# Softmax normalised in the exponent, spectrum and its swapped copy in one slot, and new instruction orders, in a four-layer attention and state-space kernel

## The chip, the cores and the metric

The kernel runs on one core of one Trainium2 chip. The metric is device time in microseconds (us) of one execution. The engines are named as the profile names them: PE (TensorE, matmuls), PEld (its weight loads), DVE (VectorE), ACT (ScalarE), POOL (GpSimd) and SP (SyncE, which issues nearly all DMAs).

## The reference, cut to what matters

Four residual layers on x of 2048 rows by 512 columns in bf16: attention (A), long convolution (B), A, B, each fed by a layer norm. The same weights serve both layers of a kind.

```python
def A(x, wqkv, wo):                      # 32 heads of 16, window of 8 keys, every second row
    q, k, v = split(x @ wqkv)
    idx = pos[:, None] - 2 * arange(8)[None, :]
    logits = einsum("bhsd,bhswd->bhsw", q, k[idx]) * 16 ** -0.5    # -1e9 where idx < 0
    return einsum("bhsw,bhswd->bhsd", softmax(logits), v[idx]) @ wo

def B(u, A_re, A_im, B_re, B_im, C_re, C_im, log_dt, Dskip):
    K = einsum("dn,dnl,dn->dl", C, exp(dt * A * l), dt * B).real   # 512 kernels of length 2048
    return irfft(rfft(u, 4096) * rfft(K, 4096))[:2048] + u * Dskip

x = x + A(layernorm(x)); x = x + B(layernorm(x))
x = x + A(layernorm(x)); x = x + B(layernorm(x))
```

## The kernel before, in words

Everything stays in SBUF between the layers; the residual is `x_sb`, 128 partitions by 16 rows by 512. There is no scheduler at work: `manual_schedule` keeps each engine's instructions in the order in which Python emits them, and that order comes from strings of letters. `ORDERK` orders the first stage, `CORE0` and `CORE1` the two attention layers, `ORDER0`, `ORDERF` and `ORDER1` the two convolutions and the way from the first to the second attention layer. One letter is one piece of work: usually a few matmuls and the instruction that empties their PSUM tile. Because each engine takes its queue in order, a letter's place decides what its instructions wait behind.

Five stages follow each other:

- **First stage** (`k_gen`, `ORDERK`). The convolution kernel K is made from powers of exp(dt A), by complex products on DVE (`tt`, L1108) and matmuls (`product`, L1266); the layer norm, the transposes and the q and k projections of the first attention layer run beside it.
- **First attention core** (`core`, `CORE0`). For each of four blocks of 512 rows: `mult` (L340) forms the products of q with eight shifted views of k on DVE, four instructions of 4096 elements; `lsum` (L348, L352) sums them on PE into a logits tile `L` of two PSUM banks, of which there are two. Blocks 0 and 1 are laid out with heads on partitions, blocks 2 and 3 with rows on partitions. Then the softmax, below. `pv_mult` (L465) multiplies the weights with eight shifted views of v on DVE, one instruction of 4096 elements for each of 16 groups of rows, `pv_sum` (L480, L490) sums on PE into `po`, ACT copies to `oT`, and `out_proj` (L499, L501) applies wo and adds the residual. `v_proj` (L396, L398), `q_proj` (L221, L223), `out_proj` share two PSUM tiles `pq`. `CORE0` also carries the load and rearrangement of K (`k_part`, L1448) and the sines of the last transform (L732).
- **First convolution** (`FftB.run`, `ORDER0`), two groups of columns. Letters: K and U are the first transform step of the kernel and of the data (`f1`, L799), k and u the second (`f2`, L806), m the product of the two spectra (`u_mult`, L852), y and Y the first inverse step (`i1`, L883, and L879 for Y, which uses whole rather than split matmuls), z, v and w the last step with the residual (`i2`, L907 to L914; `i2_cols`, L927 to L933; w takes eight rows by 128 columns, v four by 128, z four by 256). Each of these ends by emptying a PSUM tile; the last letter, A or D, says whether ACT or DVE does it (`evac`, L788). The u tiles are always emptied by ACT (L865).
- **Way to the second attention core** (`ORDERF`, and the first letters of `CORE1`): the rest of z, v and w, layer-norm statistics (`half_stats`, L148, as soon as half the columns of four rows are there), transposes (L269) with their copies (L271, by the letter's engine), the k and q projections (L280, L283), the shifted copies of k (L293).
- **Second attention core and second convolution** (`CORE1`, `ORDER1`), as the first ones, with the kernel's spectrum read back from DRAM (`u_mult`, L849).

The softmax of a block, by letters: x is the maximum over the window (`mx`, L412, DVE). e is `sub_exp`: two matmuls with minus the identity subtract the maximum in `L` (L423), and ACT exponentiates with the scale 1/4 into `ex` (L424). r is `recip`: eight matmuls sum `ex` over the window into the front of `L` (L431), and ACT takes the logarithm and then the exponential of its negative (L437, L438), which is the reciprocal. n is `norm_p`: DVE multiplies `ex` by the reciprocal (L443 for blocks 0 and 1, L446 for blocks 2 and 3). T, for blocks 0 and 1 alone, turns the result by eight transposes (L452) into a part of `L` and copies it out on ACT (L454).

The kernel's spectrum in the first convolution: `k_f2` empties a tile into a slot of 1024 columns, `kn`. `kf_load` then makes a copy `ks` with neighbouring partitions swapped (real and imaginary part), by two DMAs into another slot of 1024. `u_mult` multiplies the data's spectrum with `kn` and with `ks`, two DVE instructions, and sends `kn` to DRAM for the second convolution. There are 12 slots at first and 8 more when the last K is done; a swapped copy is asked for when its product is at most four ahead, or when slots are plentiful (`room`).

Of the kernel before, what the change touches and what calls it, by code (L numbers as in the profile page):

```python
# [20 lines left out]
P = 128  # L21
S = 2048
# [24 lines left out]
sCiibsCbiisCiiMbMCGMiMsabiMcbiasMbbCCaGiMMTsibGGTGTicMbGsbiaTbcisbbTTTMGiiTbTiMaGsaGGTMiGacMabTl  # L47
MlMMMWMlaiMsiMayMwMiMybyaTMysteMMqatMaaMkeMadTkqMialKMMlQMkWMlaqMMcbqykTQHqUaUKqQaakUTyqUkyqUUpU
KUkyUapxUxtaUpatpeUaldHQqeUqkKUkl3TT33TQkkxpWl3KxTpTxyxTylTWTpqlkyyTqpHKkzkQzxKUtkUktezUqqeUKTkT
kQKztktkTeeKkUkUKTTkkKUUUkUxUUpxEUpkxpUkUUkpEKkKqxpkUxoxpEoKXqUokUkQUpKxpZxXxZXZ  # L50
"""
ORDER0 = """
KD KA KA KA KD KA KD KA KD KA KD kA kD kA kA kD UA KD UA UD kA UA kD UA KD UA
UD UA KD kA u UD m UA KA u UD u UD m KA u kA m m UA u u kD m m u
UA u UD kA m UA kD kA u m kA kD u kA yA m YD m u m u YA u u m u
yA m m u yA m m YA yA yD yD
# [3 lines left out]
yA yA z01D yA z00D yA yD h00 yA h01 YA v100A v110A v102A v013A h10 a0 p0 n0G z02A v111A v101A S v112A  # L60
h02 h11 T0 E00A a1 E01A z13D p1 n1G v003A P03 Q00 h12 a2 P01 T1 E10A p2 P00 E11D n2G h03 P11 P12
P13 T2 E20A h13 a3 E21D P02 p3 n3D P22 P21 P10 T3 E30D E31D P23 P20 x1
"""
ORDER1 = """
UA UD UA UD UA UA UD UA UD UA UD u UD u u UA m u m u m UA m u m u
UD m m UA u m u m u u yA YA u m m u yD m YA m u u m m u yA
YA m yA YD w000D yA yA yD yA z03D yA w010D yA yD yA z02D v103A v113D v112D v102D v110D v100A v111D v101A
# [3 lines left out]
vvmvvlvmvvmlvxlemvrmnlqmqvlTvqlxevqmlvmvmPvvP1rnllxS0qTmqOeVmrqP4qSl2OPPSOSOPSmPP5On3l8ml6SPCOOV  # L71
AlxSPP7eOSrObSPn9POSdOESOPSPbDadBPfaGOtFOaaawVfHSbatO
"""
CORE1 = """
0m1l2ml3mvvqqlmmlmvqqvvllxmemqvlrnvvlmxTqqlvvmqlmvPvvvvmvqlleqVPrmxqmnqSTOePlPmSOPllSPOSPrOSnOPS
mOSPOblxOSPPdeOSrffbVPdfwOnPfVOPSOSPafbOPSdafftOSafatO
# [4 lines left out]
KROWS = "ADDAADAA"  # L81
# [3 lines left out]
def build_a_consts(nc, cpool, tpool, c):  # L85
# [112 lines left out]
class LayerA:  # L198
# [158 lines left out]
    def core(self, x_sb, u, lnp, order, ev, nprod=0):  # L357
# [3 lines left out]
        scale = float(DH) ** -0.5  # L361
# [5 lines left out]
        with ExitStack() as c2:  # L367
# [45 lines left out]

            def sub_exp(q):
                L, m = st[q]["L"], st[q]["mx"]
                ex = wk.tile([P, W * P], BF16, name="ex", bufs=1)[:]
                ex = ex.rearrange("c (w p) -> c w p", w=W) if q < ncol else ex.rearrange("p (a w h) -> p a w h", a=4, w=W)
                for j in range(2):
                    if q < ncol:
                        o, r = L[:, 4 * j:4 * j + 4], m.unsqueeze(1).to_broadcast([P, 4, P])  # L420
                    else:
                        o, r = L[:, 2 * j:2 * j + 2], m[:, 2 * j:2 * j + 2].unsqueeze(2).to_broadcast([P, 2, W, H])
                    nc.tensor.matmul(o, lhsT=nident[:], rhs=r, start=False, stop=True, skip_group_check=True)  # L423
                nc.scalar.activation(ex, L[:], ACT.Exp, scale=scale)  # L424
                st[q]["ex"] = ex

            def recip(q):
                ex, L = st[q]["ex"], st[q]["L"]
                tot = L[:, 0, :] if q < ncol else L[:, 0, 0:4, :]
# [3 lines left out]
                ssum = wk.tile([P, P], F32, name="ssum")[:]  # L433
                rs = st[q]["rs"] = wk.tile([P, P], BF16, name="rs", bufs=1)[:]
                if q >= ncol:
                    ssum = ssum.rearrange("p (a h) -> p a h", h=H)
                nc.scalar.activation(ssum, tot, ACT.Ln)  # L437
                nc.scalar.activation(rs if q < ncol else rs.rearrange("p (a h) -> p a h", h=H), ssum, ACT.Exp, scale=-1.0)  # L438

            def norm_p(q):  # L440
                ex, rs = st[q]["ex"], st[q]["rs"]
                if q < ncol:
                    nc.vector.tensor_tensor(ex, ex, rs.unsqueeze(1).to_broadcast([P, W, P]), ALU.mult)  # L443
                    return
                attn = st[q]["attn"] = wk.tile([P, 4, W, H], BF16, name="attn", bufs=2)
                nc.vector.tensor_tensor(attn[:], ex, rs.rearrange("p (a o h) -> p a o h", o=1, h=H).to_broadcast([P, 4, W, H]), ALU.mult)  # L446
# [144 lines left out]
    def spare(self):  # L591
# [4 lines left out]
        return [r[:, i * n:(i + 1) * n].rearrange("p (q e) -> p q e", e=EC) for r in rest for i in range(r.shape[-1] // n)]  # L596
# [141 lines left out]
class FftB:  # L738


    def __init__(self, tc, nc, C, ident, w2_dram, g2_dram, kf_dram, x_sb, tag):
# [9 lines left out]
        self.kf, self.nat, self.ub, self.cnt = {}, {}, {}, {}  # L751
# [5 lines left out]
    def open_mid(self):  # L757
# [9 lines left out]
        if not t:  # L767
            self.free = list(self.spare) + [self.wk.tile([P, DQG, EC], BF16, name="kf_sb")[:] for _ in range(3)]
# [40 lines left out]
    def k_f2(self, g, ec, eng):  # L809
        n = g * NEC + ec  # L810
        p2 = self.f2(g, "ka", ec)
        kf = self.nat[n] = self.free.pop(0)
        self.evac(kf, p2, eng)
        self.nk += 1
        self.pump()

    def open_ring(self):
        kp2 = self.ring_pool.tile([P, 8, DQG, EC], BF16, name="kf_nat", tag="kp")
        self.free += [kp2[:, i] for i in range(8)]

    def room(self):
# [757 lines left out]
```

## Time and profile before

| what | value |
|---|---|
| time, median of 3 runs | 402.94 us (402.64 to 403.21) |
| the profiled execution's own time | 402.72 us |
| its span, first to last instruction | 400.8 us |
| last DVE instruction ends | 396.7 us |
| granted TensorE clock | 0.999 |
| DMA | 54.17 MB, mean 135 GB/s |

The span of the profiled execution is 1.9 us shorter than its own time, which also holds what lies before the first and after the last instruction. A row of the view of groups reads: line, engine, operation, output and inputs by the program's names, sizes, count, then busy time and the mean duration of one in ns, then the idle time of the engine just before these instructions and what ended it. The durations of two DVE or ACT instructions in a row overlap a little; where it matters, the distance from start to start is used, from the timeline. The table of stretches gives for each stretch its length, then the busy time of PE, PEld, DVE, ACT and POOL.

### The profile page before, as it was taken

Reading aid. Unit: us, or ns where it says so; the run is one execution under the profiler, and the core shown is the slowest. Engines: PE = TensorE matmul, PEld = TensorE weight load, DVE = VectorE, ACT = ScalarE, POOL = GpSimd, SP = SyncE. Lnnn points to the kernel's source line nnn. Section 1 sums busy time; section 2 is a strip of 40 time slices with the busy share of each in tenths; the row PEclk is TensorE's granted clock in tenths of the full one; section 3 lists DMA queues with packets and bytes.
Section 4 is the critical chain, followed back from the end, with each engine's and each line's share of the span. In section 5 each row is a group of like instructions: output and inputs, shape, how many; then the busy total and the mean of one; then the engine's idle time right before and its main releaser. Section 6 shows DMA issues by size and latency. Waiting matters only on the chain.

```text
span 400.8 us, 14761 instructions
## 1 busy us (share of the span) xinstructions
PE 320.0 (80%) x6479; PEld 227.6 (57%) x6527; DVE 381.5 (95%) x475; ACT 326.0 (81%) x565; POOL 66.1 (17%) x79
## 2 busy tenths in 40 slices
PE   3000178789999899889997889999999998998795
PEld 2000037557635567656887878643456766667785
DVE  6999999999999999999999999979999999989995
ACT  7999999786656499888999998864655788989983
POOL 9402500000299600030500002300000001000000
PEclk9999999999999999999999999999999999999999
DMA  7942820323014855285235677740063009504606
GB/s 220 395 132 31 87 65 12 83 54 94 12 39 110 216 180 152 79 296 225 101 115 206 223 270 215 263 136 2 2 169 94 3 20 404 162 2 108 213 11 205
DMA packets 62322, 54.17 MB, mean 135 GB/s; under 512 B 33869, under 2 KB 50738, under 8 KB 60978
## 3 DMA queue, kind: packets, MB, share of 16 engines
q1 hardware_dynamic: 62250, 53.22, 43.6%
q8 instruction: 51, 0.84, 0.9%
q14 instruction: 13, 0.11, 0.1%
q10 hardware_dynamic: 8, 0.00, 0.0%
HBM read 30.15 MB, written 13.24 MB: 108 GB/s over the span
## 4 chain that ended last, share of the span: by engine, by line
PE 29%; DVE 21%; issue 9%; ACT 7%; DMA 4%; SPq 1%; POOL 0%; DVEq 0%; ACTq 0%
DVE pav L465 5%; PE pq L396 5%; PE pq L501 4%; PE po L490 4%; DVE prod L340 3%; PE pq L221 3%; DVE t L849 3%; DVE t L852 3%; DVE ln_bn L148 2%; PE pb L799 2%; DMA v_ext<-v_ext 2%; PE L L352 2%; DVE a1s L788 1%; PE pb L806 1%; PE pb L883 1%
## 5 line engine op out<-in xcount | busy, mean ns | idle before, releaser
L465 DVE TENSOR_TENSOR pav<-attn,v_ext 128x4096 bf16<-128x4096 bf16 (+1 forms) x34 | 72.6, 2169 | 0.2
L340 DVE TENSOR_TENSOR prod<-qT,kT_ext 128x4096 bf16<-128x4096 bf16 x29 | 66.6, 2322 | 0.4 <-ACT qT L223 0.3
L1108 DVE TENSOR_TENSOR A_t<-A_t,pow_t 128x1024 bf16<-128x1024 bf16 (+4 forms) x46 | 37.9, 870 | 0.2
L1194 PE MATMUL pt<-ident,x_blk 128*128 128x128 bf16 x64 | 6.3, 241 | 39.6 <-ACT x_blk L193 39.6
L501 PE MATMUL pq<-wop,oT 128*128 128x512 bf16 x122 | 31.7, 379 | 3.4 <-issue 2.5
L490 PEld LDWEIGHTS <-pav 64*128 64x128 bf16 x1664 | 26.0, 95 | 13.4 <-DVE pav L465 6.0
L490 PE MATMUL po<-ident,pav 64*128 64x64 bf16 x1664 | 29.0, 190 | 4.2 <-DVE pav L465 2.3
L865 ACT CAST ub<-pb 128x1024 bf16<-128x1024 f32 x32 | 31.9, 1068 | 0.2
L398 ACT CAST v_ext<-pq 128x512 bf16<-128x512 f32 x32 | 18.8, 586 | 16.1 <-PE pq L396 16.1
L1204 PE MATMUL pp<-xnT,kT_ext 128*128 128x512 bf16 x88 | 25.3, 404 | 7.8 <-ACT qT L1209 2.8
L806 PE MATMUL pb<-a1s,w_sb 128*128 128x64 bf16 x768 | 27.3, 193 | 5.0 <-ACT a1s L788 3.1
L396 PE MATMUL pq<-wv,xnT 128*128 128x512 bf16 x120 | 29.9, 379 | 0.4
L806 PEld LDWEIGHTS <-w_sb 128*128 128x128 bf16 x768 | 24.8, 98 | 7.2 <-issue 4.8
L1194 PEld LDWEIGHTS <-x_blk 128*128 128x128 bf16 x64 | 4.7, 107 | 42.0 <-ACT x_blk L193 40.4
L788 DVE CAST a1s<-pb 128x1024 bf16<-128x1024 f32 x21 | 24.7, 1214 | 2.5 <-PE pb L799 2.2
L788 ACT CAST a1s<-pb 128x1024 bf16<-128x1024 f32 x27 | 26.4, 1043 | 0.8 <-PE pb L799 0.8
L1266 PEld LDWEIGHTS <-A_t 128*64 128x64 bf16 (+1 forms) x512 | 21.9, 103 | 4.7 <-DVE A_t L1108 0.6
L1266 PE MATMUL pk<-B_t,A_t 128*64 128x84 bf16 (+1 forms) x512 | 23.7, 201 | 1.0 <-ACT kgs L1274 0.5
L221 PE MATMUL pq<-xnT,kT_ext 128*128 128x512 bf16 x92 | 23.0, 379 | 0.2
L176 POOL TENSOR_TENSOR ln_rstd<-ln_rstd,ln_mh 128x4 f32<-128x4 f32 x2 | 4.0, 2016 | 107.4 <-DVE ln_rstd L175 107.4
L396 PEld LDWEIGHTS <-xnT 128*128 128x128 bf16 x128 | 11.7, 97 | 14.3 <-issue 1.7
L492 ACT CAST oT<-po 128x512 bf16<-128x512 f32 x26 | 14.9, 575 | 5.8 <-PE po L490 5.8
(261 smaller groups left out, 902.9 us busy)
## 6 DMA issues: line engine op xcount, KB each, us to landing
w_sb<-w_dram SPq DMA_DIRECT2D x8, 1024.0 KB, 6.8
w_dram<-xnT SPq DMA_DIRECT2D x1, 4096.0 KB
kf_ring<-kf_dram SPq DMA_DIRECT2D x13, 256.0 KB, 4.5
kf_ring<-kf_dram SPq DMA_DIRECT2D x26, 128.0 KB, 3.9
v_ext<-v_ext SPq DMA_DIRECT2D x4, 784.0 KB, 6.4
x_blk<-in_A_x_dram SPq DMA_DIRECT2D x4, 512.0 KB, 4.7
kT_ext<-in_A_wqkv_dram SPq DMA_DIRECT2D x4, 512.0 KB, 9.5
x_sb<-in_A_x_dram SPq DMA_DIRECT2D x4, 512.0 KB, 6.1
```

The lines of the kernel that those rows point to most:

```text
L221: nc.tensor.matmul(pq[:], lhsT=self.wqk[:, dt, ft * P:(ft + 1) * P], rhs=self.xnT[:, dt, q * 512:(q + 1) * 512], start=(dt == 0), stop=(dt ...
L340: nc.vector.tensor_tensor(pr, self.qT[q][:, ft].unsqueeze(1).to_broadcast([P, W, 4, P]), kap, ALU.mult)
L396: nc.tensor.matmul(pp[:], lhsT=xnT[:, dt, a * P:(a + 1) * P], rhs=wv[:, dt, :], start=(dt == 0), stop=(dt == NDT - 1))
L465: nc.vector.tensor_tensor(pv[:, i], attn[:, n % 4].unsqueeze(2).to_broadcast([P, W, DH // parts, H]), vap, ALU.mult)
L490: nc.tensor.matmul(po[:, h, 0, i * nt + ft, :], lhsT=pvf[rows, i, w, ft * P:(ft + 1) * P], rhs=ident[rows, rows], start=(w == 0 and ft + i ...
L501: nc.tensor.matmul(pw[:], lhsT=oT[:, ftp, :], rhs=self.wo[:, ftp, :], start=False, stop=(ftp == NDT - 1))
L788: (self.nc.scalar.copy if eng == "act" else self.nc.vector.tensor_copy)(dst, src)
L806: nc.tensor.matmul(p2[:, j, :], lhsT=self.w2[:, ec * EC + j, :], rhs=a1s[:, ec * EC + j, :], start=True, stop=True)
L865: nc.scalar.copy(ub[:], p2)
L1108: return lambda: nc.vector.tensor_tensor(*args)
L1204: nc.tensor.matmul(pps[kind, b, ft][:], lhsT=la.wqk[:, dt, c:c + P], rhs=la.xnT[:, dt, b * 512:(b + 1) * 512], start=(dt == 0), stop=(dt = ...
L1266: nc.tensor.matmul(o, lhsT=lhs, rhs=Bt[:, ri, c * CH + ql].rearrange("p b g -> p (b g)"), start=(not half and j % 4 == 0 and ri == 0), sto ...
```

## The change

The logits' scale of 1/4 moves from the exponential into the indicator matrices that sum the products over a head. The normalisation is done in the exponent: after the sum, ACT takes its logarithm (less half the logarithm of 8, for the rounding to bf16), PE subtracts that from `L` by two more matmuls, and ACT exponentiates `L` a second time, straight into the weights. The sum is now made in a `pq` tile, since `L` must keep the logits. The DVE multiplication by the reciprocal is gone.

A slot of the first convolution now holds the spectrum and its swapped copy side by side (2 by 1024 columns): five pairs at first, four more when the last K is done. The copy is asked for as soon as the spectrum is there, and one DVE instruction of 2048 elements makes both products.

All six order strings are new, with the engine letters in them. The engines of several copies and applies in the first stage become tables (`ENGK`), of the copies of K too (`KROWS`), with other values: seven of the eight `k_part` copies are on DVE, where three were.

```diff
-KROWS = "ADDAADAA"
+ENGK = dict(b="AAAAAAAAAAAAAAAAA", y="DAAAAAAAADAA", z="DAAA", e="AAAAAAAA", K="AAAAAAAAAAAAAAAA", Q="AAAAAAAA", x="AAAAAAAAAAAAAAAA")
+KROWS = "DADDDDDD"
...
-        nc.gpsimd.tensor_scalar(m1[:], u[:], 0, None, ALU.is_ge)
+        nc.gpsimd.tensor_scalar(m1[:], u[:], 0, float(DH) ** -0.5, ALU.is_ge, ALU.mult)
...
+            def less(q, r):
+                L = st[q]["L"]
+                for j in range(2):
...
+                    nc.tensor.matmul(o, lhsT=nident[:], rhs=b, start=False, stop=True, skip_group_check=True)
             def sub_exp(q):
...
-                nc.scalar.activation(ex, L[:], ACT.Exp, scale=scale)
+                less(q, st[q]["mx"])
+                nc.scalar.activation(ex, st[q]["L"][:], ACT.Exp)
             def recip(q):
-                tot = L[:, 0, :] if q < ncol else L[:, 0, 0:4, :]
+                tot = pq_tile()[:, 0:P]
+                ls = wk.tile([P, P], BF16, name="ls")[:]
...
-                nc.scalar.activation(ssum, tot, ACT.Ln)
-                nc.scalar.activation(rs if q < ncol else rs.rearrange("p (a h) -> p a h", h=H), ssum, ACT.Exp, scale=-1.0)
+                nc.scalar.activation(ls, tot, ACT.Ln, scale=math.exp(-centre))
             def norm_p(q):
-                    nc.vector.tensor_tensor(ex, ex, rs.unsqueeze(1).to_broadcast([P, W, P]), ALU.mult)
...
-                nc.vector.tensor_tensor(attn[:], ex, rs.rearrange("p (a o h) -> p a o h", o=1, h=H).to_broadcast([P, 4, W, H]), ALU.mult)
+                less(q, st[q]["ls"])
...
+                nc.scalar.activation(out, st[q]["L"][:], ACT.Exp, bias=-centre)
...
-        while self.nkf < self.nk and (self.nkf < self.nm + self.ahead or self.room()):
+        while self.nkf < self.nk and (self.tag == 0 or self.nkf < self.nm + self.ahead):
...
-            kn, ks = self.nat[n], self.free.pop(0)
+            kc = self.kf[n]
             for h in range(2):
-                sync.dma_start(ks[h::2], kn[1 - h::2])
+                sync.dma_start(kc[h::2, 1], kc[1 - h::2, 0])
...
-            for i, k in enumerate((kn, ks)):
-                self.nc.vector.tensor_tensor(t[:, i], ub[:], k, ALU.mult)
+        self.nc.vector.tensor_tensor(t, ub[:].unsqueeze(1).to_broadcast([P, 2, DQG, EC]), kc, ALU.mult)
```

The orders of the two cores, before and after:

```diff
-CORE0 vvmvvlvmvvmlvxlemvrmnlqmqvlTvqlxevqmlvmvmPvvP1rnllxS0qTmqOeVmrqP4qSl2OPPSOSOPSmPP5On3l8ml6SPCOOV
-      AlxSPP7eOSrObSPn9POSdOESOPSPbDadBPfaGOtFOaaawVfHSbatO
+CORE0 vvvmvvlmqvqlxmevvlrmvlvnmlvmmTvqxllvqvvmqPemvqSrllPmqxn1OT0meVPrlP5S3POSqmOl2SPOSPOm4PlSlb7xn6O8
+      VOePSOdrAPSPPDnOSOSPCO9SbPOwHfPGVOfbPdFSBOEftSataaOfa
-CORE1 0m1l2ml3mvvqqlmmlmvqqvvllxmemqvlrnvvlmxTqqlvvmqlmvPvvvvmvqlleqVPrmxqmnqSTOePlPmSOPllSPOSPrOSnOPS
-      mOSPOblxOSPPdeOSrffbVPdfwOnPfVOPSOSPafbOPSdafftOSafatO
+CORE1 0m1l2ml3mqqqlqmvvlmvvvmxqlemvvllrmvmnqlTqqmxvlmlevvvvqPvvvlmrPqlSnmmxOqSPTqeSPOPSlPOOmlSPrbSmnOP
+      SOwPllxdSOOVefPaaPaSrOnVPbOSOPSdPOPbVaOSdfOPatfaSfataO
```

In the last letters of the way to the second core and of the end, `ORDERF` no longer has a z: the last step of the first convolution is done by v and w alone, and blocks 2 and 3 get their layer-norm statistics by whole rows (H2, H3) rather than by half rows (h). The two z of `ORDER1` are v and w too:

```diff
-ORDERF yA yA z01D yA z00D yA yD h00 yA h01 YA v100A v110A v102A v013A h10 a0 p0 n0G z02A ... T3 E30D E31D P23 P20 x1
+ORDERF yD yA yA yA yD yD YA w010A v101A v111A v110A h00 v100A h01 h11 w001A h10 a0 ... T3 P20 E31D P21 E30D x1
-ORDER1 ... YD w000D yA yA yD yA z03D yA w010D yA yD yA z02D v103A v113D v112D v102D v110D v100A v111D v101A
+ORDER1 ... w001D yA yA w010D yA yA yA yA YD w011D YA v101D v102D v112D v111D v100A v110D v113A v103D
```

In the built programs DVE has, against before, 8 normalisations fewer (8 to 0), 16 spectrum products instead of 32 in the first convolution, 7 copies of K instead of 3, 7 copies of transposed tiles in the second attention layer instead of 4, and 16 half-row and 14 whole-row statistics instead of 32 and 6. PE has 16 matmuls of 512 columns more (`L` from `ls`), and ACT 8 exponentials of 1024 elements more and 8 instructions of 128 elements fewer.

More of the change, by code (lines that the diff above doesn't have):

```diff
@@ L595, in spare @@
         n = DQG * EC
[L596 removed]
+        return [r[:, 0:2 * n].rearrange("p (k q e) -> p k q e", k=2, e=EC) for r in rest]
     def ring_extra(self):
@@ L767, in open_mid @@
         if not t:
-            self.free = list(self.spare) + [self.wk.tile([P, DQG, EC], BF16, name="kf_sb")[:] for _ in range(3)]
+            self.wk2 = self.c_mid.enter_context(tc.tile_pool(name="b0_wk2", bufs=1, reuse_waits="tile"))
+            self.free = list(self.spare) + [self.wk2.tile([P, 2, DQG, EC], BF16, name="kf_sb")[:]]
     def gtile(self, name):
@@ L817, in open_ring @@
     def open_ring(self):
[L818 to L822 removed]
+        kp2 = self.ring_pool.tile([P, 4, 2, DQG, EC], BF16, name="kf_nat", tag="kp")
+        self.free += [kp2[:, i] for i in range(4)]
     def pump(self):
[L825 removed]
+        while self.nkf < self.nk and (self.tag == 0 or self.nkf < self.nm + self.ahead):
             self.kf_load(self.nkf)
```

120 lines of the change are left out of this document (59 added, 61 removed).

## The prediction

> **What bounds the kernel now.** I read the page's busy times first, then the same by stretches, then the groups by form for prices, last the waits and the timeline for what ends idle time. The page:
>
> ```profile
> span 400.8 us, 14761 instructions
> ...
> PE 320.0 (80%) x6479; PEld 227.6 (57%) x6527; DVE 381.5 (95%) x475; ACT 326.0 (81%) x565; POOL 66.1 (17%) x79
> ```
>
> DVE has 381.5 of 400.8 us. Of its 19.3 idle us some 4 lie before its work gets going and 4.1 after its last instruction (it ends at 396.7). So the first account is of DVE. The table of stretches (length, then PE, PEld, DVE, ACT, POOL): first stage, first core, first convolution, way to the second core, second core, second convolution.
>
> ```profile
> 0.00:109.60 109.60, 56.84 (x711) 38.72 (x721) 104.93 (x172) 95.81 (x177) 23.65 (x49) 1.00 0.42 108
> 109.60:188.80 79.20, 71.42 (x1461) 45.19 (x1476) 78.59 (x61) 59.79 (x120) 30.05 (x15) 1.00 0.53 160
> 188.80:240.00 51.20, 44.79 (x1359) 40.52 (x1358) 48.25 (x65) 49.65 (x58) 6.04 (x8) 1.00 0.51 183
> 240.00:269.10 29.10, 28.35 (x360) 19.93 (x362) 25.69 (x74) 22.52 (x40) 5.38 (x7) 1.00 0.68 218
> 269.10:357.00 87.90, 83.67 (x1553) 51.16 (x1573) 85.43 (x72) 62.46 (x134) 1.02 (x1) 1.00 0.30 98
> 357.00:400.80 43.80, 34.93 (x1050) 32.12 (x1044) 38.60 (x36) 35.78 (x40) 0.00 (x0) 1.00 0.42 123
> ```
>
> In the first stage and the cores DVE never stops for long. In the convolutions three engines are almost equally full, and on the way to the second core PE is (28.35 of 29.10). There the time follows DVE only in part.
>
> **Prices.** Groups by form (busy, mean ns of one, idle before):
>
> ```profile
> L849 DVE TENSOR_TENSOR t<-ub,kf_ring 128x2048 bf16<-128x2048 bf16 x13 | 15.1, 1215 | 0.0
> ...
> L424 ACT ACTIVATE ex<-L 128x1024 bf16<-128x1024 f32 x8 | 8.2, 1019 | 4.3 <-PE L L423 4.3
> ...
> L852 DVE TENSOR_TENSOR t<-ub,kn 128x1024 bf16<-128x1024 bf16 x12 | 7.6, 683 | 0.0
> ...
> L443 DVE TENSOR_TENSOR ex<-ex,rs 128x1024 bf16<-128x1024 bf16 x4 | 3.1, 784 | 0.0
> ...
> L446 DVE TENSOR_TENSOR attn<-ex,rs 128x1024 bf16<-128x1024 bf16 x4 | 2.7, 682 | 0.0
> ...
> L271 DVE COPY xnT<-pt 128x1024 bf16<-128x1024 bf16 x4 | 2.6, 673 | 0.9 <-PE pt L269 0.8
> ...
> L438 ACT ACTIVATE rs<-ssum 128x128 bf16<-128x128 f32 x8 | 2.5, 310 | 0.3
> ```
>
> Neighbours overlap by some 0.08 us, so I count start to start. The timeline shows it:
>
> ```profile
> 323.49 0.68 DVE L446 TENSOR_TENSOR attn<-ex,rs 128x1024 bf16<-128x1024 bf16 x1
> 324.09 2.28 DVE L465 TENSOR_TENSOR pav<-attn,v_ext 128x4096 bf16<-128x4096 bf16 x1
> ```
>
> 0.60, not 0.68. In the same way 1.14 for 1215 ns, 0.63 for 673 ns, and on ACT 0.93 for 1019 ns.
>
> **The change part by part, on DVE.**
> - Normalisation gone: 3.1 + 2.7 less 8 overlaps of 0.08 = 5.2 us, half in each core.
> - Spectrum products: 32 x 0.60 = 19.2 become 16 x 1.14 = 18.2: -1.0. The row of 683 ns suggests more than twice that; the overlap takes it away.
> - Copies of K, 4 more at 0.33 (row L1448 on DVE: 412 ns): +1.3, in the first core.
> - On the way to the second core 3 more transposed copies at 0.63: +1.9. Layer-norm applies at 0.33 to 0.45: one fewer in the first stage, two fewer in the first core, two more on the way, four more in the second core: +1.2.
> - Tiles of the convolutions: emptied one more by DVE, +1.1, but of the last step 5 x 1.16 become 3 x 0.60 and 2 x 1.14: -1.7.
> - Statistics: 16 half rows at 0.33 for 8 whole rows at 0.60: -0.5.
>
> Sum -2.9; by stage: first stage -0.3, first core -2.6 + 1.3 - 0.6 = -1.9, first convolution and the way +2.2, second core -2.6 + 1.3 = -1.3, second convolution -1.8 (one tile and 0.6 of residual adds), which with roundings is -3.1.
>
> **On ACT and PE.** For each block ACT gains a second exponential of 1024 elements, 0.93 by row L424, and drops an exponential of 128, 0.30: +2.5 a core. Its bias may be read from a pointer; ACT applies with two pointers take 804 ns where the sum of squares (L143) without takes 630, so +0.09 each at most, nothing at least; I take nothing. With the moved copies, applies and residual tiles ACT comes to +0.7, +0.2, -3.9, -0.4, +1.4 by the five stages. In both cores it stays 20 us below DVE, which hides it. PE gets two matmuls of 512 columns per block, 0.216 start to start (rows L423, L501): +1.7 a core, up to 2.4 if each pair also waits for its logarithm. Three more inverse tiles are whole: 16 matmuls at 0.056 = 0.90 against 32 split ones at 0.0175 = 0.56, so 0.35 each; 20 more identity matmuls cost at most 1.1. POOL, 17% busy, has two applies fewer.
>
> **The wait that is added.** PE's second subtraction waits for ACT's logarithm; behind it in PE's queue stand projections, `lsum`, `pv_sum`. In the orders one to three letters (0.86 us for a projection, 1.1 for an `out_proj`) lie between r and n, against 0.2 to 1.0 for ACT to get to a logarithm of 0.28. So 0 to 0.4 us a block, on PE. DVE waits for the weights at the first P of a block; between n and it lie at least one P or m (2.2 us) against 0.43 + 1.0 for subtraction and exponential, except before P of block 2 in the first core, where a table load of 1.28 comes in between and P, x and two small ones (3.8) cover about 3.9. I count 0.3 for all of it; bounds 0 and 2. A logits tile is held until the second exponential rather than the logarithm, some 1.5 us longer; `lsum` of the block after the next comes later than that in every case. The `pq` tile for the sum is free again after the logarithm: nothing, at most 0.3 a block.
>
> **The slots.** Swapped copies are now queued on SP directly behind each tile. While slots are refilled, a k runs five to eight tiles ahead of its m, far over what one landing takes here. Before, emptying a tile sometimes waited for the slot's last store, in the chain in order of time:
>
> ```profile
> 210.07 3.62 DMA kf_dram<-w_sb
> ...
> 220.28 4.22 DMA kf_dram<-kn
> ```
>
> Now a pair is taken again after 9 tiles at most; from an m to the k that takes its pair, DVE has at least five instructions of 1.14, 5.7 us, against 0.6 of issue and 4.2 of landing. The waits of 0.8 (DVE) and 0.5 (ACT) should go; if not, each of seven reuses could cost up to 0.8.
>
> **The sum by stage.** First stage: -0.2. First core: DVE is 78.6 of 79.2, so -1.9 + 0.1 = -1.8. First convolution and the way: DVE +2.2, of its 6.4 idle I give 1.2 back (the slot waits): +1.0; bounds -1.5 and +4.8. Second core: DVE -1.3, but PE goes from 83.7 to 85.4 of 87.9: -0.9; bounds -1.5 and +0.5. Second convolution: DVE -1.8, but ACT rises from 35.8 to 37.2 and becomes the fullest, and its last tiles now come four in a row: 0.0; bounds -1.5 and +1.3. Together -1.9 on 402.7, the profiled execution's own time (span 400.8 and 1.9 around it; the median of the runs, 402.94, is 0.2 higher): **400.8 us**.
>
> **Rivals.**
> 1. DVE's time passes through in full, -3.1, and the slot waits' 1.3 go too: 398.3. For it: no idle of DVE over 0.2 us from 279 to 353. Against it: PE at 95% of the second core. [...] Chance 0.20.
> 2. PE becomes the bound of the second core: its +1.7 is added to what DVE loses there; no gain there, the second convolution +0.7 through ACT: 402.7 - 0.2 - 1.8 + 1.0 + 0.0 + 0.7 = 402.4. The chain runs over PE's `pv_sum` and `out_proj` from 310 to 330, which speaks for it. Chance 0.16.
> 3. Slower: the way to the second core turns into DVE's chain. Each of seven transposed copies stands in DVE's queue behind PE's transposes, where four did; the one that waited cost 0.8. Three more at 0.85 are 2.6, on top of +2.2: +4.8 instead of +1.0, and 404.6. It decides from +4.0 there (400.8 + 3.0 is 0.2% over the median). Against it: PE, not DVE, is full in that stretch now. Chance 0.24.
> 4. That the change does not do what it says can nearly be left out: the order of instructions has the eight multiplications gone.
>
> **How the numbers follow.** The forecast, 400.8 with its own range of 399.6 to 402.1, has 0.40, rival 1 0.20, rival 2 0.16, rival 3 0.24. About 0.2% (0.8 us) is what a measurement can tell from no change here. Faster: 0.60; within: 0.16; slower: 0.24. The range goes from 397.4 (rival 1 with the best bound of the first convolution) to 405.0 (rival 3 and a bit of slot waits).
>
> **What would show it.** DVE busy of 378 to 379, ACT near 324, PE up by 4 to 7; the first core 1.5 to 2 us shorter; no DMA store ending a wait of DVE or ACT in the first convolution; ACT fuller than DVE after the second core. Wrong: DVE idle above 22, above all between the last product and the first `mult` of the second core, or `pav` instructions waiting for `attn`.

## The result, and the profile after

The changed kernel takes 408.58 us (median of three runs, 407.41 to 409.22), the kernel before beside it on the same chip 403.07: ratio 1.0126, 95% interval 1.0105 to 1.0147. (Single runs that no trace explains, one each of after and gap_split at 1122 us, of gap_wlate at 831 and of gap_pad64 at 416, are in none of the medians and ratios here.) The forecast was 400.8, in a range up to 405.0. The profiled execution has an own time of 408.58 and a span of 406.8, 6.0 more than before.

The page after, busy times:

```profile
span 406.8 us, 14843 instructions
...
PE 334.3 (82%) x6559; PEld 233.5 (57%) x6559; DVE 377.3 (93%) x454; ACT 324.6 (80%) x556; POOL 57.0 (14%) x77
```

DVE's work fell by 4.2 us (381.5 before), more than the 3.1 that the forecast had by stages. Its idle time rose from 19.3 to 29.5. (PE's rise is partly in the records: before lacks 48 of its matmuls, after none.) The table of stretches of the kernel after, cut where each stage ends on DVE (first `mult` of a core, first emptied tile of a convolution; first convolution and way are one row):

```profile
0.00:111.20 111.20, 61.36 (x729) 39.74 (x730) 104.93 (x171) 96.52 (x178) 24.43 (x52) 1.00 0.42 107
111.20:192.20 81.00, 76.95 (x1488) 47.74 (x1488) 75.96 (x58) 61.18 (x120) 19.69 (x13) 0.98 0.54 163
192.20:273.40 81.20, 73.55 (x1726) 61.31 (x1721) 74.75 (x121) 67.56 (x90) 9.93 (x13) 1.00 0.55 186
273.40:361.70 88.30, 86.95 (x1563) 51.52 (x1563) 84.31 (x71) 62.07 (x129) 2.92 (x1) 1.00 0.30 97
361.70:406.80 45.10, 35.49 (x1072) 33.15 (x1066) 37.34 (x35) 37.30 (x41) 0.00 (x0) 0.99 0.40 120
```

| stage | before | after | forecast | measured | DVE busy |
|---|---|---|---|---|---|
| first stage | 109.60 | 111.15 | -0.2 | +1.55 | 0.0 |
| first core | 79.17 | 81.06 | -1.8 | +1.9 | -2.55 |
| first convolution and way | 80.34 | 81.17 | +1.0 | +0.8 | +0.8 |
| second core | 87.85 | 88.35 | -0.9 | +0.5 | -1.1 |
| second convolution | 43.88 | 45.07 | 0.0 | +1.2 | -1.3 |

The last cut is not quite the same place in both: the old `ORDER1` gives its first tile to ACT, the new one to DVE. Cut at the first tile that either engine empties, the second core goes from 87.40 to 88.35 (+0.95) and the second convolution from 44.33 to 45.07 (+0.74).

Every stage has its own new waits. DVE's in the whole execution (total, times, longest):

```profile
DVE z L796 <- PE pb L879: 1.7, 1, 1.7
DVE prod L342 <- PE L L350: 1.7, 1, 1.7
...
DVE pav L472 <- PE po L487: 1.6, 1, 1.6
...
DVE prod L342 <- ACT v_ext L400: 1.0, 2, 0.5
```

No `pav` waits for `attn`: the wait that the change adds, weighed so long in the prediction, costs DVE nothing, and PE waits 0.2 us in all for the logarithm. The long waits stand elsewhere: the first `prod` (1.74 us at 111.15), the last `pav` of the first core (1.61 at 184.70), a tile `z` of the second convolution (1.7). The chain around the second of these:

```profile
178.07 0.65 PE pq L508 x3
178.72 2.14 issue
180.87 0.55 PE pq L508
181.41 3.25 PE po L487 x32
```

PE stops for 2.14 us between two matmuls of one `out_proj`, and nothing that the profile shows holds it. Behind the stop the granted clock is 0.5 for 3.4 us, and the same 32 matmuls of `pv_sum` that took 1.95 before take 3.46. The row of after, then those of before, whose one stop at this place is of 0.85:

```profile
181.20 3.46 PE L487 MATMUL po<-ident,pav 128*128 128x128 bf16 x32
```

```profile
180.58 1.02 PE L490 MATMUL po<-ident,pav 64*128 64x64 bf16 x58 [0.85 <-issue]
...
183.70 1.95 PE L480 MATMUL po<-ident,pav 128*128 128x128 bf16 x32
```

### The profile page after: what moved, and what is told of

Its sections match the earlier page's. It is cut to its first block, busy times and chain, and to the rows that moved or that the text cites. A ratio compares the mean times of both kernels' runs of the same rounds, so it can differ in the third digit from the quotient of the medians.

```text
span 406.8 us, 14843 instructions
## 1 busy us (share of the span) xinstructions
PE 334.3 (82%) x6559; PEld 233.5 (57%) x6559; DVE 377.3 (93%) x454; ACT 324.6 (80%) x556; POOL 57.0 (14%) x77
## 4 chain that ended last, share of the span: by engine, by line
PE 43%; DVE 29%; ACT 14%; issue 8%; DMA 4%; POOL 1%; SPq 0%; DVEq 0%; ACTq 0%; POOLq 0%
PE pq L398 7%; DVE pav L472 7%; PE pk L1273 6%; PE pq L223 4%; PE pp L1211 4%; DVE prod L342 3%; DVE B_t L1115 3%; PE pq L508 3%; PE pp L282 3%; ACT ub L865 3%; PE po L497 3%; DVE t L852 3%; DVE A_t L1115 2%; PE L L350 2%; PE pb L883 2%
## 5 line engine op out<-in xcount | busy, mean ns | idle before, releaser
L508 PE MATMUL pq<-wop,oT 128*128 128x512 bf16 x128 | 33.2, 380 | 2.3 <-issue 2.1
L1211 PE MATMUL pp<-xnT,kT_ext 128*128 128x512 bf16 x96 | 28.5, 425 | 5.7 <-ACT kT_ext L1216 3.6
L796 ACT CAST a1s<-pb 128x1024 bf16<-128x1024 f32 x30 | 28.7, 1046 | 1.7 <-PE pb L807 1.6
L1273 PE MATMUL pk<-B_t,A_t 128*64 128x84 bf16 (+1 forms) x512 | 24.6, 206 | 0.0
L223 PE MATMUL pq<-xnT,kT_ext 128*128 128x512 bf16 x96 | 24.0, 380 | 0.0
L796 DVE CAST a1s<-pb 128x1024 bf16<-128x1024 f32 x18 | 21.5, 1217 | 2.4 <-PE pb L807 2.2
L225 ACT CAST qT<-pq 128x512 bf16<-128x512 f32 x24 | 14.1, 586 | 10.5 <-PE pq L223 10.5
L514 ACT ACTIVATE x_sb<-pq 128x512 bf16<-128x512 f32 x24 | 14.3, 595 | 8.8 <-PE pq L508 8.3
```

The source lines that it names most:

```text
L223: nc.tensor.matmul(pq[:], lhsT=self.wqk[:, dt, ft * P:(ft + 1) * P], rhs=self.xnT[:, dt, q * 512:(q + 1) * 512], start=(dt == 0), stop=(dt ...
L508: nc.tensor.matmul(pw[:], lhsT=oT[:, ftp, :], rhs=self.wo[:, ftp, :], start=False, stop=(ftp == NDT - 1))
L796: (self.nc.scalar.copy if eng == "act" else self.nc.vector.tensor_copy)(dst, src)
L1211: nc.tensor.matmul(pps[kind, b, ft][:], lhsT=la.wqk[:, dt, c:c + P], rhs=la.xnT[:, dt, b * 512:(b + 1) * 512], start=(dt == 0), stop=(dt = ...
L1273: nc.tensor.matmul(o, lhsT=lhs, rhs=Bt[:, ri, c * CH + ql].rearrange("p b g -> p (b g)"), start=(not half and j % 4 == 0 and ri == 0), sto ...
```

## The experiments

All ratios are to the kernel before, on the same chip. "Gap" means the changed kernel with the wider filler tile of the first experiment; most others build on it. The times of the profiles are stage lengths cut as above, of one execution of each kernel. How far they can be trusted shows the second core: it is the same in eight of the builds, and takes 88.33 to 89.46. The slots alone under the old `ORDER0` could not be tried: that order holds more spectra at once than five pairs.

**The halves of the change.** newnorm is before with the new normalisation alone (newnorm_gap with the wider tile as well), oldnorm the changed kernel with the old normalisation, conv_new before with the new slots, `ORDER0` and `ORDERF` alone.

```diff
 newnorm:  before  + less(), sub_exp(), recip(), norm_p() and the scaled indicators of the change
 oldnorm:  after   - recip(), norm_p() of the change, + those of before
 conv_new: before  + spare(), class FftB, ORDER0, ORDERF of the change
```

newnorm: 

> The kernel before, with the normalisation in the exponent alone: old orders, old slots. The multiplication by the reciprocal (5.2 us of DVE) goes, the layout shifts as in the changed kernel. Theory that the orders are to blame: 403 - 5.2 + 1.7 for the layout + up to 1 for PE, 399.5 to 401. Theory that the normalisation itself costs, because PE becomes the bound of the cores: 403 to 406.

newnorm_gap: 

> As the run before it, with the gap tile widened by 768 bytes. Orders to blame: 398 to 399.5, that is 1.2 to 1.8 us less than without the wider gap. Normalisation to blame: 402 to 404.5.

oldnorm: 

> The changed kernel with the old reciprocal and the DVE multiplication put back, everything else as changed. Orders to blame: DVE gets 5.2 us back where it is full, less 1.7 of layout, so 410 to 413. Normalisation to blame: PE gets 3.4 us and its waits back, 403 to 406.

conv_new: 

> The kernel before with only the slots of the change (spectrum and swapped copy side by side, one product of 2048 elements) and the new orders of the first convolution and of the way to the second core; normalisation, first stage, both cores and the end are those of before. Theory (the loss comes with the cores; the convolution's own gain of 1 us on DVE is eaten by ACT and PE): cores within 0.5 of before, first convolution and way 80.3 to 81.3 against 80.34, 402.8 to 404.3 in all. Rival 1 (slots and order gain where the core before them is not late): first convolution 78.5 to 79.8, 401 to 402.5. Rival 2 (the way and the second core of different orders do not fit each other): second core 1.5 us or more longer, 405 to 408.

Measured: newnorm 413.04, ratio 1.0247 (1.0224 to 1.0269); newnorm_gap 411.93, 1.0221 (1.0191 to 1.0251); oldnorm 415.23, 1.0302 (1.0272 to 1.0333); conv_new 405.71, 1.0059 (1.0032 to 1.0086). All but conv_new are slower than both full kernels and above every range that was expected of them: neither half alone is to blame, normalisation and orders fit each other in pairs. In newnorm DVE has 3.4 us less in the first core, which is 5.1 longer. DVE's waits in both cores (the first line stands in the first core):

```profile
DVE mx L412 <- PE L L330: 4.7, 1, 4.7
DVE pav L470 <- ACT attn L451: 4.1, 2, 3.4
```

Under the old orders the wait for `attn` is real, 4.1 us, of which 3.4 in the second core; under the new ones it is gone. conv_new keeps the cores (first 79.44, second 87.39), so the second core does not suffer from the new way into it (rival 2); its first convolution and way take 82.68 against 80.34, more than either expectation of that stage, and 1.2 of that is a stop of PE like the one above.

**Layout and the end of the first `mult`.** In the changed kernel the first core's work pool is smaller (the two f32 sums and `rs` are gone, two smaller `ls` have come), and the tile `prod` lies where the last product of the first stage lies. So it waits for the last logits sum. The filler tile moves it.

```diff
 gap:       -wk.tile([P, 1680], BF16, name="gap")   +wk.tile([P, 2064], BF16, name="gap")
 gap_p0:    CORE0 ...vvmqPemvqSr...  ->  ...vvmqemPvqSr...        (the first P one e and one m later)
 gap_split: one product of 2048  ->  two of 1024, first convolution
 gap_end:   ORDER1 of before
 gap_w:     CORE0: w (load of 4 MB) ahead of the second half of K
```

gap: 

> The changed kernel with the unused gap tile of the first core widened from 1680 to 2064 elements, by the 768 bytes that the softmax no longer needs, so that the first product tile lies where it lay before. Layout theory: the 1.7 us wait of the first core's first product for the last sum of the logits goes, and the kernel is 1.2 to 1.8 us faster than the changed one (some 406.5 to 407.5). Rival: PE is behind there anyway, the wait comes back at the next product or at the first weighted values, and the time stays within 0.5 us of the changed kernel's.

gap_p0: 

> The changed kernel with the wider gap tile, and in the first core's order the first P moved behind the next e and m (from 'mqPemvq' to 'mqemPvq'). Theory that the first weighted values wait for the shifted copy of v, whose DMA stands in SP's queue behind 24 stores of K: the 1.95 us wait at 133 is filled by a product, and the first core ends 1.5 to 2 us earlier; against the wider gap alone -1.2 to -2. Rival: PE is the pace of the first core, DVE only waits later: within 0.5 of the wider gap.

gap_split: 

> The changed kernel with the wider gap tile, and each product of the first convolution made by two instructions of 1024 elements again, on the two halves of the pair. By the start-to-start distances 16 x (2 x 0.60 - 1.14) = 1.0 us more of DVE. Theory that DVE sets that stage: +0.7 to +1.2. Rival, that PE and ACT set it: within 0.3.

gap_end: 

> The changed kernel with the wider gap tile and the old order of the second convolution (ORDER1 of before). Theory that the new order, which gives ACT four tiles in a row near the end and DVE less work, is to blame for the 1.2 us that the last stage lost: the last stage is 43.9 again, -0.8 to -1.3 against the wider gap. Rival: the stage pays for the way it is entered: no change.

gap_w: 

> The changed kernel with the wider gap tile, and the load of the 4 MB of transform weights issued before the second half of K instead of behind it. Theory that PE's 2 us stop at 181 with no cause in the trace is a late fetch of its own instructions, while the weights' load takes the DMA engines: the load moves some 10 us earlier, the stop at 181 goes or moves to 165 to 175, and if it goes the time falls by 1 to 2 us. Rival: the stop belongs to the place in PE's program: it stays at 181 and the time is the same, or more as the second half of K comes later.

Measured:

| run | us (range) | ratio (interval) | what moved |
|---|---|---|---|
| gap | 407.79 (406.44 to 410.04) | 1.0128 (1.0084 to 1.0173) | first stage 109.47, first core 81.60 |
| gap_p0 | 407.49 | 1.0100 (1.0069 to 1.0131) | wait at P gone, others of 0.4 to 0.6 in its place; first core 82.12 |
| gap_split | 407.52 | 1.0094 (1.0060 to 1.0128) | DVE +1.0, stage 80.81 against 80.79 |
| gap_end | 408.13 | 1.0110 (1.0074 to 1.0145) | second core and convolution 133.94 against 133.24 |
| gap_w | 414.38 | 1.0291 (1.0254 to 1.0328) | K late: DVE waits 6.84; PE's stop at 180 gone |

The layout's 1.74 us is a real wait, and gap's first stage is 1.7 shorter, but in all little comes back (0.8 in the medians, nothing in the ratios): the first P then waits 1.95 us for the shifted copy of v, where it waited 0.67.

```profile
133.19 2.29 DVE L472 TENSOR_TENSOR pav<-attn,v_ext 128x4096 bf16<-128x4096 bf16 x1 [1.95 <-DMA v_ext<-v_ext]
```

That copy is issued by SP behind 24 stores of K (0.66 each). Before the change nine products stood ahead of the first P, now eight and no normalisation: DVE is early at a place where a DMA sets the time. gap_split: DVE's work in the first convolution may grow by 1.0 us at no cost, so it is not its bound; the 1.0 that I credited to the joined products is worth nothing there. With the old end order the last two stages together are 0.7 longer, not shorter (the cut between them falls one tile later there), so the new order is not to blame.

**What is DVE's time worth?** The cut I could make without touching the orders is the maximum: in gap_nosub DVE still computes it, but PE doesn't subtract it; in gap_nomax it is left out too; before_nomax is the kernel before without it. The weights stay the same up to rounding, as long as no logit is too large for the exponential.

```diff
-    less(q, st[q]["mx"])                     gap_nosub, gap_nomax   (before_nomax: its two matmuls)
-    nc.vector.tensor_reduce(st[q]["mx"], ..., ALU.max)              gap_nomax, before_nomax
```

gap_nosub: 

> The changed kernel with the wider filler tile, without the subtraction of the maximum from the logits (DVE still computes the maximum, nobody reads it; the sum's logarithm is centred on 2.75 instead of half the logarithm of 8). PE has 16 matmuls of 0.216 us fewer, 3.5 us, and each block's chain is shorter by two of them and by the maximum. Theory (in the cores PE and the chain over PE set the time, DVE does not): first core -0.5 to -1.5, second core -1.2 to -1.7, 404.7 to 406.0. Rival (DVE still sets the cores' time): within 0.5 of the kernel with the wider filler tile, 407.3 to 408.3.

gap_nomax: 

> As the kernel without the subtraction, and the maximum itself is left out too: DVE has 8 reductions of 1.13 us fewer, 9.0 us. The weights are the same up to rounding. Theory (DVE's time is worth little in the cores once PE and the chain set them): at most 1.5 us faster than the kernel without the subtraction, 403.2 to 405.5. Rival (DVE is the bound and its time passes through): 7 to 9 us faster than that kernel, 396 to 400.

before_nomax: 

> The kernel before, with nothing of the change, but without the maximum and its subtraction (softmax weights are the same up to rounding): DVE 8 x 1.13 = 9.0 us less, PE 16 x 0.216 = 3.5 us less, and no wait of the exponential for them. Theory A (as the prediction read the page: DVE bounds both cores of the kernel before, with 0.6 us of idle time in the first and 0.4 in the second): 394.5 to 397.5. Theory B (DVE, PE and ACT are interlocked by the orders, and DVE's time soon stops counting, as in the changed kernel, where the same cut gave 2.6): 399.0 to 401.5.

Measured: gap_nosub 406.56, 1.0082 (1.0061 to 1.0103); gap_nomax 405.22, 1.0052 (1.0021 to 1.0083); before_nomax 403.18, 0.9992 (0.9975 to 1.0008). Leaving out the maximum takes 8.3 us off DVE's busy time in the changed kernel (9.0 was the estimate), and the time falls by 1.3, less than the intervals can tell apart. In the kernel before it takes off 7.4, with an estimated 3.5 of PE's work, and the time stays. gap_nomax is where the theory put it, gap_nosub 0.6 above its theory's range, before_nomax above the ranges of both. By stage:

| stage | gap | gap_nosub | gap_nomax | before | before_nomax |
|---|---|---|---|---|---|
| first core | 81.60 | 80.89 | 79.70 | 79.17 | 76.75 |
| its DVE | 76.08 | 76.30 | 72.42 | 78.57 | 75.29 |
| first convolution and way | 80.79 | 81.61 | 80.75 | 80.34 | 83.34 |
| second core | 88.36 | 87.70 | 87.58 | 87.85 | 86.78 |
| its DVE | 84.33 | 84.33 | 79.95 | 85.40 | 81.24 |

In the second core the two matmuls of each block are worth 0.66, and 4.4 us of DVE 0.12. Beside the spread of that stage (1.1) it is clear that DVE's time is worth little there; that PE, or the chain over its matmuls, sets the time is likely, not shown. In the first core of the kernel before, -3.3 of DVE's work, together with two matmuls a block, gave -2.4, which fits DVE as the bound there, as I had read it; no run takes away the one without the other. But the next stage, in which nothing was changed, became 3.0 longer. PE's waits there, before_nomax, then PE's two stops in its timeline:

```profile
PE pb L921 <- issue: 2.0, 1, 2.0
...
PE pb L901 <- issue: 1.0, 1, 1.0
```

```profile
238.99 0.28 PE L901 MATMUL pb<-xnT,g_sb 128*128 128x256 bf16 x1 [0.99 <-issue]
...
244.91 0.23 PE L921 MATMUL pb<-z,g_sb 128*128 128x128 bf16 x1 [2.03 <-issue]
```

**The way to the second core.** From the start of the last product to the first `mult` it takes 35.5 us against 33.1; from its end 34.25 against 32.42, since the joined product is itself 0.5 longer. In the new order block 0's normalisation stands behind a tile and 16 half-row statistics of two blocks, so I put them closer.

```diff
 gap_f1, ORDERF:
-yD yA yA yD yD YA w010A v101A v111A v110A h00 v100A h01 h11 w001A h10 a0 v112A S a1 p0 p1 n0D w011A
+yD yA w010D yA yD yD YA h00 h01 v100A v110A v101A v111A h10 a0 p0 n0D w001A h11 v112A S a1 p1 w011A
```

gap_f1: 

> The changed kernel with the wider filler tile and another order on the way to the second core: the tile w010 comes four inverse steps earlier and goes to DVE, the half-row statistics of group 0 (h00, h01) stand directly behind the inverse steps, and block 0 is normalised (a0, p0, n0) ahead of the statistics of block 1. Theory (the way is longer by 2.6 us because block 0's normalisation waits for w010 behind four tiles on ACT and for 16 half-row statistics of both blocks): the first transpose 1.2 to 2.5 us sooner after the last inverse step, the stage 78.5 to 79.8 us instead of 80.8, and 405.3 to 406.8 in all. Rival (PE is full on the way, 28 of 29 us, and sets its end whenever the first transpose comes): the stage within 0.4 of 80.8, 407.4 to 408.2.

Measured: 407.10, 1.0096 (1.0073 to 1.0119); the stage 80.90 against 80.79. The theory falls, the rival holds for the stage (the total lies between their ranges). From the end of the last product on, PE is busy 32.34 of 34.4 us after the change and 31.60 of 32.5 before: 0.7 more work (165 matmuls of the last step in it where 132 were) and 1.2 more idle time. The idle time of after holds a wait of the first transposes for DVE and a stop with the cause "issue" that before does not have:

```profile
PE pt L271 <- DVE xn L197: 0.8, 1, 0.8
...
PE pb L883 <- issue: 0.5, 1, 0.5
```

With the 0.5 of the product itself, these terms cover the 2.4 us, as far as PE's rows tell.

**PE's stops.** First the load that runs during the stop at 180 us, held back until a copy of K is done (by a tiny DMA ahead of it on SP that needs this copy). gap_wlate2 is the same kernel as gap_wlate; its profile is the one that is read.

```diff
-"w": lambda: la.load_w2(w2_dram)
+"w": lambda: [nc.sync.dma_start(gate[:], kp[0:1, 96, 0, :]), la.load_w2(w2_dram)]     (w behind G in CORE0)
```

gap_wlate: 

> The changed kernel with the wider filler tile, and the 4 MB load of the second transform's table held back until copy G of K is done: about 182 us instead of 173. Theory (PE's stop of 1.9 us near 180, whose cause reads issue, comes from that load, and what follows it at the end of the first core hangs on it): no stop over 1 us between 175 and 184, the first core 79.3 to 80.0 us instead of 81.6, and 405.3 to 406.3 in all. Rival 1 (the stop belongs to that place in PE's program): it stays, 407.3 to 408.3. Rival 2 (it moves with the load into the first transform, 184 to 194 us): a stop of 1 us or more there, and at most half of the gain, 406.5 to 407.5.

gap_wlate2: 

> The same kernel as gap_wlate, for a profile that can be read. The theory there (the stop goes with the load): no PE stop over 1 us between 175 and 184, the first core 79.3 to 80.3 us. Rival 1 (it belongs to the place in the program): a stop of 1.5 us or more there, first core 81 to 82. Rival 2 (it moves with the load): a stop of 1 us or more between 184 and 196. The seven times of gap_wlate, 406.9 in the middle, lie between the two.

Measured: 406.55, 1.0085 (1.0051 to 1.0119), and 406.47, 1.0089 (1.0061 to 1.0118). The stop at 180 is gone, the first core 80.30 (gap: 81.60), and a stop of 1.44 us ends at 197.7, behind a block that had to wait in the load's new time (it is issued from 183.2 on), and a little later than expected. It moves with the load: rival 2. (The execution that was profiled, 408.53 us, is the longest of four.)

Then 19 profiles together (all but that of gap_wlate), those of the next three runs included: 18 show 33 stops of over 0.55 us with the cause "issue" after 109 us. Each ends 1.23 to 1.60 us after a transfer of 16,384 bytes of the instruction queue (q8 on the page) has landed. In the 2.5 us before that transfer begins, packets fill 95% or more of the DMA engines' time at 30 of the 33. And where the trace has all of PE's records, the number of PE instructions (matmuls and weight loads) ahead of the stop leaves the rest 181 to 183 on division by 256:

| kernel | stop ends at, us | length | PE instructions ahead | modulo 256 |
|---|---|---|---|---|
| after | 180.9 | 2.14 | 4023 | 183 |
| before_nomax | 178.3 | 0.66 | 4021 | 181 |
| before_nomax | 239.0 | 0.99 | 7093 | 181 |
| before_nomax | 244.9 | 2.03 | 7349 | 181 |
| gap_wlate2 | 197.7 | 1.44 | 4791 | 183 |

q8 moves 51 blocks in after, which has 13,118 PE instructions: 51 x 256 = 13,056. With the rest of 183, a 52nd block is asked for at 183 + 51 x 256 = 13,239. Of the padded kernels below, bn_pad64 (13,150 PE instructions) has 51 transfers, gap_pad64 (13,246) and bn_pad128 (13,278) have 52. It is PE's program that is loaded, in blocks of 256. In the trace of after PE passes an end of a block at 174.5. The next transfer usually begins 0.6 to 0.9 us later (median of each trace); here it begins at 178.4, while the 4 MB load fills the DMA engines. The DMA view, between 174.5 and 178.4 us, and between 178.4 and 179.5 (queue: packets, MB, share):

```profile
q1 hardware_dynamic: 207, 1.56, 95.0%
```

```profile
q1 hardware_dynamic: 67, 0.46, 101.7%
q8 instruction: 1, 0.02, 5.6%
```

PE reaches the next end at 178.72 and goes on at 180.87. If that is it, instructions that do nothing, put where PE is idle, must shift the stops: by half a block away from their matmuls, by a whole block back to them.

```diff
 in the first stage, ahead of the first transposes (PE is idle there from 7 to 44 us):
+            for _ in range(64 if len(xps) == 1 else 0):          # bn_pad128: 128
+                nc.tensor.transpose(pt[:, 0, 0, :], ident[:], ident[:])
 bn_pad64, bn_pad128: on before_nomax; gap_pad64: on gap
```

bn_pad64: 

> The kernel before without the maximum, with 64 transposes more (128 PE instructions, half a page of 256) in the 37 us in which PE has nothing to do in the first stage; the work after them is the same. Theory (PE stops at the end of a page of its program whose successor is late, because its 16 KB wait behind large loads): the stops at 238.0 to 239.0 and 242.9 to 244.9 us vanish from those matmuls, page ends now falling near 236.6 and 241.5, just ahead of the loads; the first convolution and way 80.5 to 81.8 us instead of 83.3, 400.0 to 401.8 in all. Rival (the stops belong to those matmuls or their data): same places, 402.7 to 403.7.

bn_pad128: 

> The same with 128 transposes (256 instructions, a whole page). Theory: the page ends fall on the same work as without them, so the stops come back at the same matmuls (0.7 to 1.3 and 1.6 to 2.4 us), 402.7 to 403.7 in all. Rival (the added transposes themselves change something, or the stops come by chance): no stops there, or others.

gap_pad64: 

> The changed kernel with the wider filler tile and the 64 transposes. Theory: the stop of 1.9 us at 179 to 181 us goes or falls below 0.8, since the page end comes some 2 us earlier, ahead of the 4 MB load; first core 79.4 to 80.4 us instead of 81.6, 405.5 to 407.0 in all, unless another page end now meets a load on the way to the second core. Rival: stop and time as without them, 407.3 to 408.3.

Measured: bn_pad64 **399.46** (398.73 to 401.83), 0.9924 (0.9903 to 0.9946); bn_pad128 402.86, 1.0005 (0.9981 to 1.0030); gap_pad64 411.25, 1.0191 (1.0162 to 1.0221). The first convolution and way of before_nomax and of bn_pad64, in the tables of stretches:

```profile
186.40:269.70 83.30, 73.52 (x1720) 60.42 (x1719) 73.93 (x138) 72.16 (x98) 11.42 (x15) 1.00 0.55 189
```

```profile
185.80:266.60 80.80, 73.62 (x1720) 60.65 (x1719) 73.96 (x139) 72.27 (x99) 11.45 (x15) 1.00 0.58 195
```

The same work, 2.5 us apart, as the theory had it (the total is a little under its range); bn_pad64 has no stop over 0.55 us after 109 us. (With the transposes the clock's record begins earlier, at 8.1 us, and reads 0.5 from 15.0 to 52.5. The first stage's length stays: 109.70 against 109.63.) In bn_pad128 the stops of 0.66 and 0.99 are back at the same matmuls (4021 + 256 and 7093 + 256 instructions) with 1.11 and 0.51; the third, of 2.03, is not, against the expectation. Its total is that of before_nomax all the same, with 1.5 us more in the first core, of which the stop is 0.45. gap_pad64 took the stop at 181 from 1.94 to 0.61 and the first core to 79.07 (with a stop of 0.81 at 159.7), and met the loads of the second layer's weights instead:

```profile
PE pb L883 <- issue: 4.4, 2, 4.1
```

One of the two is 4.07 us long and ends at 242.5: first convolution and way 85.28 against 80.79, and 2.7 more behind them, which no stop of this kind explains. So 64 transposes in idle time made one kernel faster, from 403.18 to 399.46 us (2.7 by the ratios), and another slower, from 407.79 to 411.25 (2.5 by the ratios, whose intervals just touch). bn_pad64 beats both kernels of this study; it has nothing of the change in it, and no maximum.

## Why the prediction was wrong

**The step that failed** is "First core: DVE is 78.6 of 79.2, so -1.9 + 0.1 = -1.8", and its like in the second core. DVE's work did fall: by 2.55 and 1.1 in the cores where 1.9 and 1.3 were counted, by 4.2 in all. The saving did not reach the time: DVE's idle time rose from 0.6 to 5.0 us in the first core and from 2.5 to 4.0 in the second.

- **First stage**, -0.2 forecast, +1.55 measured. I priced the edits and not the smaller pool, which put `prod` on a tile still being read. gap shows it: 109.47 without the wait.
- **First core**, -1.8 forecast, +1.9 measured. That DVE is hardly idle there in the kernel before was read rightly. Of its 5.0 us of idle time after the change, 0.67 is the wait for the copy of v, and 4.0 are four waits behind PE's stop. That stop is 1.3 longer than the one before (2.14 against 0.85), and the half clock behind it costs 1.5 (3.46 against 1.95). Two of these terms are borne out by a run: in gap_pad64, with the stop at 0.61 and the wait for v at 0.41, the core takes 79.07, which is 2.5 less than in gap, where they were 1.94 and 1.95. It is still 1.7 more than the forecast, and what holds that rest is not shown. The wait for v was foreseeable: the forecast credited time that DVE saves ahead of the first P, where a DMA ends later. The stop was not, in its size: the rows of before show one "issue" of 0.85 at that place, and I did not ask what it was. In the traces PE's program is loaded in blocks of 16,384 bytes, 256 instructions, and most ends pass unseen (in after one stop of over 0.55 us at 46 ends behind 109 us); but a stop, at 30 of 33 behind packets that filled 95% or more of the DMA engines' time, took 0.6 to 4.1 us.
- **First convolution and way**, +1.0 forecast, +0.8 measured, but by other terms, so the number was luck. DVE's work grew by 0.8, not 2.2. Up to the start of the last product the stage is 1.5 shorter, not longer. The way is 2.4 longer. That is the place of rival 3 and about its size, not its mechanism: the transposed copies waited 1.4 us in all where 0.85 were waited for before, and not 3.4.
- **The slots.** DVE no longer waits for a store of the spectrum; ACT does, once, for 1.5 us where it waited 0.5. The forecast that no store ends a wait was half wrong.
- **Second core**, -0.9 forecast, +0.5 measured. Rival 2 is the nearer one: there is no gain, and gap_nosub and gap_nomax speak for PE (0.66 for 1.7 us of PE, 0.12 for 4.4 of DVE). DVE's work fell by 1.1 us here, and none of it passed through to the time, against rival 1. DVE's new waits there, up to 0.8 us each, are for ACT's copies `v_ext` and `qT` of PE's tiles ahead of the first P.
- **Second convolution**, 0.0 forecast, +1.2 measured, at the edge of my bounds (+1.3); 0.45 of it is the place of the cut. A tile `z` of the first inverse step waits 1.75 for PE, which had waited as long for a product. The old end order takes no less time together with the core (gap_end), so the order itself is not to blame.

The normalisation's own cost was priced nearly rightly: no `pav` waits for it, ACT 324.6 for 324 forecast, DVE 377.3 for 378 to 379. "Wrong: DVE idle above 22" was the right alarm: it is 29.5. What stays open: 1.7 of the first core, and how much of the 1.3% is PE's stops in the mean of runs rather than in this one profile; no run of the changed kernel comes back to the time of before. The sum of the stops over 0.55 us after 109 us is 2.14 there and 1.49 before.

## What to carry to other kernels

An engine at 95% is the bound of a stage only if a cut of its work shortens that stage (DVE had 95% of the kernel before; with 7.4 us less work for it in before_nomax the whole still took 403.18 us): cut something large that touches no order (here a reduction) and read the stages, before pricing a change by that engine's sum. Credit time saved ahead of a fixed event (a DMA that lands, a tile that is read) only up to that event (the first P waited 1.95 us for the copy of v in gap, 0.67 in after). In a program with thousands of PE instructions compare variants at several paddings: differences of about 1% can be the places where blocks of the program end, and not the edit (64 transposes in idle time: before_nomax from 403.18 to 399.46 us, gap from 407.79 to 411.25).

## What the runs showed of the hardware that I had not expected

- PE's program was loaded in blocks of 256 instructions during the run: q8 made 51 transfers of 16,384 bytes for the 13,118 PE instructions of after, 52 for the 13,246 of gap_pad64. A block's transfer took 0.9 to 1.9 us (0.9 to 1.5 in after). It began 0.6 to 0.9 us after PE had passed a block's end (median of each trace; 0.87 in after), up to 4.1 us after it beside large loads (3.87 in after). At the 33 stops PE had run the next 256 instructions sooner than that, and went on 1.23 to 1.60 us after the transfer's end (1.47 in after); in the dense stretches of after a block mostly lasted 4 to 6 us.
- After a stop of 2.14 us the granted clock was 0.5 for 3.4 us (after); after stops of 1.94 us (gap) and 2.55 us (gap_p0) it stayed at 1.0. In gap_p0 it was 0.5 for 3.4 us from 161.4 on, with PE busy for 95% of the 3.5 us before. So the length of a stop alone does not tell. The three executions of the changed kernel differ in this too: 407.41 with a mean clock of 1.0, 408.58 and 409.22 with 0.995.
